# Four stores of the next-to-last output chunk: from two issuing engines to three

## The chip, the cores and the metric

The kernel runs on one core of one Trainium2 chip. The metric is the device time of one execution in microseconds (us), as the median of several runs. A profile of one further execution gives the times of single instructions. The engines are named as in the profile: PE is TensorE's matrix multiplication and PEld its weight load, DVE is VectorE, ACT is ScalarE, POOL is GpSimd, SP is SyncE, which here only issues transfers and waits. A "q" behind the name (SPq, ACTq, POOLq) stands for the engine's sequencer, which waits, branches and issues transfers.

## The reference

Two blocks follow each other. For 8 batches, 8 heads, 576 tokens and 64 features per head:

```python
kv = np.einsum('bhsd,bhse->bhde', k, v)
out = np.einsum('bhsd,bhde->bhse', q, kv)
rms = np.sqrt(np.mean(out * out, axis=-1, keepdims=True) + 1e-06)
x = (out / rms * g_norm)                      # then heads are put side by side: (8, 576, 512)

gate_pre = sum(conv_w[k] * xp[:, k:k + S, :] for k in range(5))   # xp: x with 4 zero rows ahead
gate = 1.0 / (1.0 + np.exp(-gate_pre))
result = (gate * (x @ w_val)) @ w_out         # float32, (8, 576, 512)
```

## The kernel before, in words

The kernel is a list of small steps, written out by hand as the string PLAN (lines 19 to 227) and carried out one after the other by the loop at lines 881 to 887. Each step's name is one of the functions above that loop, its numbers are that function's arguments, and the numbers behind an "@" choose buffers. Every engine executes its own instructions in the order in which the steps issue them; between engines, semaphores hold an instruction back until what it reads or overwrites is ready. These waits are put in by the framework. So the order of PLAN is the order on each engine, and a transfer that an engine issues stands in that engine's line like any other instruction.

The last part of the work is the product with w_out. Batches are handled in pairs i = 0 to 3; a pair's 2 x 576 tokens make eight chunks of 128 tokens and a ninth chunk (number 8) for the two remainders of 64. Two neighbouring chunks (2p and 2p + 1) are computed together by seven fast_product steps (line 819, matmuls at line 838), a scheme that saves one of eight block products. Each fast_product adds into a PSUM bank, and fast_keep (line 842) brings the banks into the output tiles ot (128 x 512 values in float32, four buffers) by ScalarE copies (lines 850 to 854 and 861) and VectorE additions (line 848, and line 861 as a VectorE copy for the very last one). Step fast_keep 3 3 5 is the addition that completes chunk 6 of the last pair, fast_keep 3 3 6 the copy that completes chunk 7.

An ot tile goes to memory in four transfers of 32 rows each (64 KB): store (line 866) loops over the blocks j = 0 to 3 that it is given and issues each on the queue that it is given (line 870). Nearly all chunks go through SyncE. Chunk 8 of the last pair goes through store_side (line 872), that is GpSimd; it stands some steps ahead of the end. Chunks 6 and 7 of the last pair go through store_last (line 863), which splits the four blocks between SyncE and ScalarE: with n = 1 blocks 2 and 3 on ScalarE, with n = 0 blocks 0 and 1 on SyncE. The last steps of the plan are:

```python
fast_keep 3 3 1 @ 0; fast_product 3 3 5; fast_keep 3 3 4; fast_product 3 3 6; fast_keep 3 3 5;
store_last 3 6 1; store_last 3 6 0; fast_keep 3 3 6; store_last 3 7 1; store_last 3 7 0
```

So each of the two engines issues two stores of chunk 6 and two stores of chunk 7. Transfers of SyncE and ScalarE share a set of eight semaphores, those of GpSimd have eight of their own; each transfer in turn takes the next semaphore of its set and waits, if it must, until the semaphore's former transfer has landed.

After the last step the program leaves the framework's context (line 913). There every engine executes a DRAIN and reports; SyncE first waits until every transfer has landed; GpSimd, after its own DRAIN, gathers the reports of the other engines, releases them, clears the semaphores, and gathers once more.

Of the kernel before, what the change touches and what calls it, by code (L numbers as in the profile page):

```python
# [222 lines left out]
fast_keep 3 3 0 @ 1; store_side 3 8; fast_product 3 2 6; fast_keep 3 2 5; fast_product 3 3 2; fast_keep 3 2 6;  # L223
store 3 4; fast_product 3 3 1 @ 0; fast_keep 3 3 2; fast_product 3 3 3; fast_product 3 3 4; store 3 5;
fast_keep 3 3 1 @ 0; fast_product 3 3 5; fast_keep 3 3 4; fast_product 3 3 6; fast_keep 3 3 5;
store_last 3 6 1; store_last 3 6 0; fast_keep 3 3 6; store_last 3 7 1; store_last 3 7 0
"""


# [1 line left out]
def kernel(  # L231
# [11 lines left out]
    nc = tc.nc  # L243
# [12 lines left out]
    HB = P // TB  # L256
# [603 lines left out]
            last = (i, p) == (B // 2 - 1, 2 * NV - 1)  # L860
            (nc.vector.tensor_copy if last else nc.scalar.copy)(out=second[:, LOW], in_=a)

    def store_last(i, c, n):
        store(i, c, nc.scalar if n else nc.sync, range(n * HB // 2, (n + 1) * HB // 2))

    def store(i, c, queue=nc.sync, blocks=range(HB)):
        ot = st["ot", i, c]
        for j in blocks:
            bb, n = divmod(c * HB + j, NJ * HB) if c < 2 * NJ else (j // 2, NJ * HB + j % 2)
            queue.dma_start(out=rows_out[2 * i + bb, n], in_=ot[j * TB:(j + 1) * TB, :])  # L870

    def store_side(i, c):
# [5 lines left out]
        turn_x, keep_x, turn_blocks, move_blocks, halo, gate_start, gate_tap, gate_end, val_product, keep_val, gated,  # L878
        val_sums, x_sums, val_fast, val_keep, out_product, keep_out, weight_sums, token_sums, fast_product, fast_keep,
        store, store_side, store_last)}  # L880
    with tc.manual_schedule():
        set_up()
# [35 lines left out]
```

## Time and profile before

| what | value |
| --- | --- |
| time, median of 3 runs | 295.73 us (295.55 to 296.74) |
| span of the profiled execution, first to last instruction | 294.9 us |
| mean granted TensorE clock | 0.993 |
| PE busy | 287.0 us, 97% of the span |
| DVE busy | 268.7 us, 91% |
| ACT busy | 198.7 us, 67% |
| POOL busy | 120.7 us, 41% |
| stores from ot on SyncE, whole kernel | 136, median 1.7 us from issue to landing |
| the same on GpSimd | 4, median 2.1 us |
| the same on ScalarE | 4, median 2.0 us |

The profiled execution's own time is told by its span, 294.9 us; the median of the runs lies 0.83 us above it. In the profile's rows the first numbers of a timeline line are the start (counted from the span's start) and the length in us; in brackets stands how long the engine had been idle, and what ended that. In the rows of a group, "x4: 315/396/430, 290.4 to 291.7" means four instructions with the shortest, median and longest duration in ns, and the start of the first and of the last in us. Rows by stretches give the busy time of each engine, then the granted clock, the busy share of the DMA engines and the GB/s moved. The duration of a transfer's issue (DMA_DIRECT2D) is the engine's time to issue it; when its data has landed is given as "DMA to landing".

### The profile page before, as it was taken

To read this page: it belongs to the slowest core of one execution; us is meant where nothing else is said; L and a number is where in the kernel's file an instruction comes from. 1 tells how busy PE (TensorE), PEld (TensorE's weight loads), DVE (VectorE), ACT (ScalarE), POOL (GpSimd) and SP (SyncE) were. 2 spreads that over 40 slices of the span, in tenths; PEclk is the share of its full clock that TensorE was granted. 3 is DMA by queue.
4 is the path that set the end of the run, shared out by engine and by line. 5 is a ranking of instruction groups with operands and counts; after the bars stand their busy time and mean duration, and the time that the engine had idled before them with its cause. 6 is when DMAs were issued, how large, how long until landed. Compare 5 with 4: busy or idle time off the path is not lost.

```text
span 294.9 us, 8675 instructions
## 1 busy us (share of the span) xinstructions
PE 287.0 (97%) x3279; PEld 226.9 (77%) x3279; DVE 268.7 (91%) x483; ACT 198.7 (67%) x621; POOL 120.7 (41%) x131
## 2 busy tenths in 40 slices
PE   7999999999999999999999999999999999999994
PEld 3776878788887768878887767888887588788583
DVE  1699999999999999999999999999998999999812
ACT  2899999999786667867477576659588433723330
POOL 3067054854491477421881649021592072000020
PEclk9997999999999999999999999999999999999999
DMA  7999998886686766946789789534553170221344
GB/s 268 379 392 410 284 276 230 239 258 176 197 189 198 234 150 182 341 144 174 182 237 279 167 218 308 165 112 109 141 128 80 44 170 2 57 53 36 98 105 120
DMA packets 32009, 55.51 MB, mean 188 GB/s; under 512 B 6166, under 2 KB 14358, under 8 KB 31968
## 3 DMA queue, kind: packets, MB, share of 16 engines
q1 hardware_dynamic: 29328, 49.50, 57.2%
q0 software_dynamic: 1760, 3.43, 5.2%
q10 hardware_dynamic: 880, 2.03, 1.8%
q8 instruction: 26, 0.43, 0.6%
q14 instruction: 15, 0.12, 0.1%
HBM read 39.21 MB, written 9.44 MB: 165 GB/s over the span
## 4 chain that ended last, share of the span: by engine, by line
PE 94%; DMA 2%; ACT 1%; DVE 1%; issue 0%
PE bank L838 33%; PE bank L747 28%; PE bank L698 11%; PE bank L476 7%; PE bank L551 6%; PE bank L785 5%; PE bank L648 2%; DMA qs<-in_q_dram 2%; PE bank L563 2%; PE bank L515 1%; PE bank L464 0%; ACT wexp L409 0%; DVE x L626 0%; ACT sq L596 0%; DVE ss L607 0%; ACT wexp L407 0%
## 5 line engine op out<-in xcount | busy, mean ns | idle before, releaser
L617 POOL TENSOR_TENSOR rt<-ss,mhalf 128x8 f32<-128x8 f32 (+3 forms) x38 | 73.1, 1937 | 82.0 <-DVE ss L607 81.8
L686 DVE SCALAR_TENSOR_TENSOR gate<-xT,cwT,gate 128x576 f32<-128x576 f32 x128 | 100.4, 807 | 0.2
L636 ACT ACTIVATE x<-bank,rt 128x64 f32<-128x64 f32 x252 | 56.1, 375 | 3.5 <-POOL rt L617 3.2
L838 PE MATMUL bank<-wsum,w 128*128 128x256 f32 x192 | 47.3, 381 | 0.0
L669 POOL DMA_DIRECT2D xT<-y x48 | 26.6, 559 | 41.6 <-DVE gv L754 13.5
L838 PEld LDWEIGHTS bank<-wsum,w 128*128 128x128 f32 x192 | 36.0, 190 | 6.1 <-issue 0.8
L747 PE MATMUL bank<-xs,vsum 128*128 128x288 f32 x144 | 37.1, 407 | 0.0
L747 PEld LDWEIGHTS bank<-xs,vsum 128*128 128x128 f32 x144 | 27.3, 190 | 7.3
L698 PE MATMUL bank<-xT,wval 128*128 128x288 f32 x128 | 32.8, 411 | 0.0
L838 PE MATMUL bank<-wout,gv 128*128 128x256 f32 x128 | 32.3, 382 | 0.0
L698 PEld LDWEIGHTS bank<-xT,wval 128*128 128x128 f32 x128 | 24.0, 192 | 6.3
L693 ACT ACTIVATE gate<-gate 128x576 f32<-128x576 f32 x32 | 23.0, 727 | 7.9 <-DVE gate L686 7.8
L838 PEld LDWEIGHTS bank<-wout,gv 128*128 128x128 f32 x128 | 24.0, 190 | 3.5
L680 ACT ACTIVATE gate<-xT,cwT 128x576 f32<-128x576 f32 x32 | 25.2, 804 | 0.9 <-DVE gv L711 0.9
L747 PE MATMUL bank<-xT,wval 128*128 128x288 f32 x96 | 25.7, 406 | 0.0
L600 ACT ACTIVATE sq<-bank 128x256 f32<-128x256 f32 (+1 forms) x70 | 21.6, 400 | 6.0 <-PE bank L551 5.8
L711 DVE TENSOR_TENSOR gv<-gv,gate 128x576 f32<-128x576 f32 x32 | 23.5, 745 | 2.0 <-ACT gate L693 1.5
L607 DVE TENSOR_REDUCE ss<-sq 128x8 f32<-128x520 f32 (+1 forms) x40 | 24.7, 624 | 0.5 <-ACT sq L600 0.4
L848 DVE TENSOR_TENSOR ot<-bank,ot 128x256 f32<-128x256 f32 (+1 forms) x32 | 17.2, 546 | 8.4 <-PE bank L838 4.1
L747 PEld LDWEIGHTS bank<-xT,wval 128*128 128x128 f32 x96 | 18.2, 190 | 4.5
L854 ACT COPY ot<-bank 128x256 f32<-128x256 f32 x16 | 6.0, 376 | 22.6 <-PE bank L838 22.6
L551 PEld LDWEIGHTS bank<-kv,qT 64*64 64x64 f32 x1008 | 16.3, 135 | 4.8 <-issue 2.1
(91 smaller groups left out, 469.4 us busy)
## 6 DMA issues: line engine op xcount, KB each, us to landing
qs<-in_q_dram SPq DMA_DIRECT2D x96, 140.0 KB, 4.0
out_dram<-ot SPq DMA_DIRECT2D x136, 64.0 KB, 1.7
k<-in_k_dram SPq DMA_DIRECT2D x14, 576.0 KB, 4.9
v<-in_v_dram SPq DMA_DIRECT2D x12, 576.0 KB, 5.3
xT<-y POOLq DMA_DIRECT2D x48, 64.0 KB, 2.7
xT<-y SPq DMA_DIRECT2D x48, 64.0 KB, 2.7
y<-in_moe_w_val_dram SPq DMA_DIRECT2D x4, 512.0 KB, 11.9
w<-in_moe_w_out_dram SPq DMA_DIRECT2D x4, 512.0 KB, 7.1
```

The lines of the kernel that those rows point to most:

```text
L551: nc.tensor.matmul(st["raw", b, c][r][cols, to * D:(to + 1) * D], st["qT", b][rows, hp, first:first + D], kvs[b % 2][rows, hp, :], start=T ...
L607: nc.vector.reduce_sum(out=st["ss", b][:, FIRST[c]:FIRST[c] + n], in_=st["sq", b, c][:, 0:n], axis=AX.X)
L617: nc.gpsimd.tensor_tensor(out=st["rt", b][:, which], in0=st["ss", b][:, which], in1=mhalf[:, which], op=ALU.pow)
L636: nc.scalar.activation(out=x[:, to * D:(to + 1) * D], in_=raw[:, h * D:(h + 1) * D], func=AF.Copy, scale=root[:, to:to + 1])
L669: (nc.sync if i % 2 else nc.gpsimd).dma_start(out=xTs[b % 2][i * TB:(i + 1) * TB, :, first:first + P], in_=y[a * TB:(a + 1) * TB, i])
L680: nc.scalar.activation(out=gate[:], in_=xTs[b % 2][:, jt, HALO:SX], func=AF.Copy, scale=cwT[:, K - 1, jt:jt + 1])
L686: nc.vector.scalar_tensor_tensor(out=gate[:], in0=xTs[b % 2][:, jt, tap * TB:tap * TB + S], scalar=cwT[:, tap, jt:jt + 1], in1=gate[:], op ...
L693: nc.scalar.activation(out=gate[:], in_=gate[:], func=AF.Sigmoid)
L698: nc.tensor.matmul(val[:], wval[:, kc, jt * P:(jt + 1) * P], xTs[b % 2][:, kc, HALO + n * SV:HALO + (n + 1) * SV], start=(kc == 0), stop=( ...
L711: nc.vector.tensor_tensor(out=both, in0=both, in1=st["gate", b, jt][:], op=ALU.mult)
L747: nc.tensor.matmul(st[bank, "val", b, mj][:], weights_[:, k], tokens()[:, k], start=(n in (0, 1, 3) and k == 0), stop=(k == NK // 2 - 1), ...
L838: nc.tensor.matmul(st[bank, i, p], tokens()[:, k], weights_[:, k], start=(n < 2 and k == 0), stop=(k == NK // 2 - 1), skip_group_check=True)
```

## The change

PLAN's last line becomes two, and store_last takes the engine's number and the range of blocks as arguments, with GpSimd as a third engine. Of chunk 6, blocks 2 and 3 are now issued by GpSimd, block 1 by ScalarE and block 0 by SyncE. Chunk 7 is stored as before: blocks 2 and 3 on ScalarE, 0 and 1 on SyncE.

```diff
-store_last 3 6 1; store_last 3 6 0; fast_keep 3 3 6; store_last 3 7 1; store_last 3 7 0
+store_last 3 6 2 2 4; store_last 3 6 1 1 2; store_last 3 6 0 0 1; fast_keep 3 3 6; store_last 3 7 1 2 4;
+store_last 3 7 0 0 2
...
-    def store_last(i, c, n):
-        store(i, c, nc.scalar if n else nc.sync, range(n * HB // 2, (n + 1) * HB // 2))
+    def store_last(i, c, n, first, last):
+        store(i, c, (nc.sync, nc.scalar, nc.gpsimd)[n], range(first, last))
```

HB is 4, the number of blocks in a chunk. All lines behind the plan move down by one: line 870 becomes 871, and line 913 becomes 914.

## The prediction

> **What bounds the kernel now.** I read three views: the page's slices (who is busy when), the timeline of the last 12 us, and the groups of the end line L913 (what the engines do after their last instruction of the kernel's own). First two parts of the page:
>
> ```profile
> PE 287.0 (97%) x3279; PEld 226.9 (77%) x3279; DVE 268.7 (91%) x483; ACT 198.7 (67%) x621; POOL 120.7 (41%) x131
> PE   7999999999999999999999999999999999999994
> POOL 3067054854491477421881649021592072000020
> ```
>
> PE is busy in every slice but the first and half of the last, so TensorE bounds the kernel up to its last matmul. The change touches nothing before that, so its whole price lies in the tail. POOL is idle in the last slices but one; that is the free engine that the change uses. The timeline of the tail:
>
> ```profile
> 283.53 0.39 ACT L850 COPY ot<-bank 128x256 f32<-128x256 f32 x1
> ...
> 283.94 2.06 POOL L870 DMA_DIRECT2D out_dram<-ot  x4 [36.82 <-ACT ot L850]
> ...
> 289.49 1.03 PE L838 MATMUL bank<-wsum,gv 128*128 128x256 f32 x4
> 289.69 0.69 DVE L848 TENSOR_TENSOR ot<-bank,ot 128x512 f32<-128x512 f32 x1 [0.38 <-DMA out_dram<-ot]
> 290.46 1.80 ACTq L870 DMA_DIRECT2D out_dram<-ot  x4
> 290.56 0.42 DVE L861 COPY ot<-bank 128x256 f32<-128x256 f32 x1 [0.17 <-PE bank L838]
> ```
>
> Chunk 6 is ready when the DVE addition ends (289.69 + 0.69 = 290.38), chunk 7 when the DVE copy ends (290.56 + 0.42 = 290.98). Behind them stand eight 64 KB stores, four on SyncE and four on ScalarE. The timeline of SyncE alone has its four in one row; then the group of all eight, and the one for ScalarE's last:
>
> ```profile
> 290.45 1.72 SPq L870 DMA_DIRECT2D out_dram<-ot  x4
> ```
> ```profile
> L870 SPq DMA_DIRECT2D out_dram<-ot x4: 315/396/430, 290.4 to 291.7; - x4
> L870 ACTq DMA_DIRECT2D out_dram<-ot x4: 371/410/440, 290.5 to 291.8; - x4
> ...
> DMA to landing us min/median/max: 1.7/1.9/2.1
> ```
> ```profile
> L870 ACTq DMA_DIRECT2D out_dram<-ot x1: 440/440/440, 291.8 to 291.8; - x1
> ...
> DMA to landing us min/median/max: 2.1/2.1/2.1
> ```
>
> Each queue takes about 0.4 us per store, so the last is issued at 291.8 and lands 2.1 us later, at 293.9. What follows is the exit, all of line L913, from 283 us to the end:
>
> ```profile
> L913 SPq EVENT_SEMAPHORE  x11: 17/28/28, 292.2 to 294.8; - x11
> L913 POOLq EVENT_SEMAPHORE  x4: 17/17/17, 294.1 to 294.8; - x4
> L913 POOLq DRAIN  x3: 40/108/5310, 285.3 to 294.6; - x3
> L913 SPq DRAIN  x3: 7/7/7, 294.1 to 294.4; - x3
> L913 PEldq DRAIN  x2: 13/604/1195, 289.4 to 294.4; - x2
> ```
>
> SyncE waits for every landing and reports at 294.1; POOL, which gathers the reports of all engines, takes over at 294.1 (its first semaphore) and the span ends at 294.9. So 0.8 us of exit stand behind the last report. The row to stop at is POOL's DRAIN. One of the three takes 5310 ns. The same view cut to POOL and 284 to 291 us has it alone:
>
> ```profile
> L913 POOLq DRAIN  x1: 5310/5310/5310, 285.3 to 285.3; - x1
> ```
>
> It runs from 285.3 to 290.6, whereas POOL's last store issue ended at 283.94 + 2.06 = 286.00. It waits for no semaphore that the trace shows, and lasts 4.6 us past the end of POOL's last issue. The other two (108 and 40 ns, after 294) follow no store. Now this drain ends 3.5 us before 294.1 and costs nothing. The changed kernel puts two POOL stores ahead of it, at the very end.
>
> **The change part by part.** *Removed:* one store of chunk 6 from SyncE and one from ScalarE, the last of each queue's pair. In the built program each queue then has three stores: one of chunk 6, two of chunk 7. The first goes out as before (290.45, 290.46); the next must wait for chunk 7's copy, 290.98, plus the 0.07 us that lay between the addition's end (290.38) and SyncE's first issue (290.45): 291.05. Another 0.43 us for one issue (1.72 for four) puts the last at 291.48 in place of 291.8, and with the same 2.1 us to land it is down at 293.6: 0.3 us earlier than 293.9.
>
> *Added, the stores:* two issues on POOL of this kind:
>
> ```profile
> L870 POOL DMA_DIRECT2D out_dram<-ot x4: 498/504/567, 283.9 to 285.5; - x4
> ...
> DMA to landing us min/median/max: 2.0/2.1/2.4
> ```
>
> The first takes 0.57, the second 0.50, 1.07 together. When do they start? In the changed program POOL waits for DVE's addition in a separate semaphore instruction, then issues. The nearest place where a POOL store stands behind such a wait is L669; its group from 198 to 211 us:
>
> ```profile
> L669 POOL DMA_DIRECT2D xT<-y x3: 551/551/599, 209.7 to 210.8; - x3
> L669 POOLq EVENT_SEMAPHORE  x1: 11006/11006/11006, 198.1 to 198.1; - x1
> ```
>
> The wait ends at 198.1 + 11.0 = 209.1, the first issue begins at 209.7: a lead of about 0.55 us. The other bound is the store of chunk 8, which began at 283.94, right when the ACT copy before it had ended (283.53 + 0.39 = 283.92): no visible lead. I take 0.55, the like case: the wait ends at 290.4, the issues run from 290.95 to 292.0, and the second, begun at 291.5, lands 1.9 to 2.4 us later, 293.4 to 293.9. So the landings end between 293.6 and 293.9: at best 0.3 us is won, and no more, since the DMA engines are not idle meanwhile (the busy share by stretches):
>
> ```profile
> 291.50:292.00 0.50, 0.00 (x0) 0.00 (x0) 0.00 (x0) 0.00 (x0) 0.00 (x0) 1.00 0.94 262
> 292.00:292.50 0.50, 0.00 (x0) 0.00 (x0) 0.00 (x0) 0.00 (x0) 0.00 (x0) 1.00 0.89 262
> 292.50:293.00 0.50, 0.00 (x0) 0.00 (x0) 0.00 (x0) 0.00 (x0) 0.00 (x0) 1.00 0.92 275
> ```
>
> The Trainium skill, "DMA: Bandwidth & Descriptors", section "Specifications", gives about 1 us to the first byte for a GpSimd store and about 0.6 us for one of SyncE or ScalarE, which speaks against the move. By that figure, as an estimate, each moved store would land 0.4 us later after its issue. The trace has 2.1 against 1.9 us at the median, half of it; the rows decide, and the sum changes by 0.2 us in its unimportant part.
>
> *Added, the wait behind them:* queued behind the two issues on POOL is only the exit: the drain, then the gathering of all reports. Until now its cover was the 3.5 us between 290.6 and 294.1. That cover goes. The drain's price behind a late store is bounded below by its short forms, 0.04 to 0.1 us (nothing outstanding), and above by 5.3 us from its own start. I take 4.6 us past the last issue, from the one drain that follows stores. Counted the other way, from the last POOL landing (285.5 + 2.4 = 287.9, so 2.7 us to 290.6), it gives 293.4 to 293.9 plus 2.7, that is 296.1 to 296.6: the same place within 0.5 us.
>
> *Sum:* last POOL issue ends 292.0; drain to 296.6; exit 0.8; span 297.4 against 294.9, +2.5 us. The runs' median, 295.73, lies 0.83 us above the span; I carry that over: 298.2 us. With no lead on POOL the drain ends at 296.0 and the time is 297.6; with the lead and another half microsecond in drain or landing it is 298.7. Its own range is 297.4 to 298.8.
>
> **The rivals.**
>
> *The drain has no price of its own* (not slower). Then the long DRAIN at 285.3 would have ended for some other reason, and the end of the matmuls at 290.5 is suspiciously near its end at 290.6. For this: one sample only, and no semaphore. Against: PE has a drain of its own (1195 ns from 289.4) for its matmuls, POOL has none to wait for, and POOL's short drains, which come where no store is open, last 0.1 us. The mechanism left is the relief of the issuing queues, and the place where it decides is the last landing: 0 to 0.3 us earlier than 293.9, so 295.4 to 295.7 us. It decides if POOL's drain ends before 294.1, that is if it costs less than 2.1 us past the last issue. The Trainium skill has this side too: "DMA: Bandwidth & Descriptors", section "Issuing engines are not separate DMA queues", says that issuing from several engines saves just the time to issue, which is usually small. The trace agrees on the landings: 0.3 us is all that can go.
>
> *The drain works off a backlog, so much per store.* Four stores from 283.94 to the drain's end at 290.6 make 6.6 us, or 1.7 us each; two would make 3.3 us from 290.95, ending at 294.3, 0.2 us after the present gathering: 295.9 us. For this: POOL's own issues follow each other unhindered, so whatever remains is done behind them. Against: after the last landing at 287.9 no store is left to work on, and the drain still lasts 2.7 us.
>
> *The drain is longer here*, since the two POOL stores share the DMA engines with six others, all in 290.4 to 294: every microsecond of it goes into the time, 299 us or more.
>
> That the change does nothing is ruled out: the two POOL stores do stand behind chunk 8's four in the built program, and chunk 7's queues are as before.
>
> **How the numbers follow.** About 0.5% (1.5 us) is what a measurement of this kernel can tell from no change. The fixed drain: 0.68, 298.2 us. The longer one: 0.04. The backlog: 0.13, 295.9. No price: 0.15, 295.4 to 295.7. Slower by over 0.5% (above 297.2) are the first two, 0.72. The other two lie within 0.5%; a gain of 1.5 us would need the last landing at 292.4, when the stores of chunk 7 are barely issued, so 0.01 for faster and 0.27 for the same. The range that leaves out 2 in 10 takes in the forecast's own and reaches down over the backlog: 295.8 to 298.8 us.
>
> **What would show it.** In the profile after, on POOL: two more L871 issues starting at 290.9 or 291.0 (a start at 290.4 takes away the lead); a DRAIN on L914 that ends near 296.6, and POOL's gathering semaphore right behind it rather than at SyncE's report. SyncE's last wait should end at 293.7 to 294.1, well before. If the drain again ends at about 290.6 or right after the issues, the first rival holds; near 294.3, the second. If SyncE's report comes after POOL's drain, the forecast is wrong whatever the time.

## The result and the profile after

The changed kernel takes 298.31 us (median of 6 runs, 298.04 to 299.62) against 295.5 us for the kernel before (6 runs, 295.27 to 296.74). The ratio is 1.0092, with a 95% interval of 1.007 to 1.0114: it is slower by 2.1 to 3.4 us.

First the same two rows of the page, then the timeline of the tail (start, length, engine, line, what; lines are one higher than before):

```profile
PE   7989999999999999999999999999999999999990
POOL 3066064654694289224770756040890262000021
```
```profile
288.72 0.69 DVE L849 TENSOR_TENSOR ot<-bank,ot 128x512 f32<-128x512 f32 x1 [0.38 <-DMA out_dram<-ot]
289.49 1.40 ACTq L871 DMA_DIRECT2D out_dram<-ot  x3
289.59 0.42 DVE L862 COPY ot<-bank 128x256 f32<-128x256 f32 x1 [0.17 <-PE bank L839]
289.96 0.98 POOL L871 DMA_DIRECT2D out_dram<-ot  x2 [4.94 <-issue]
```

PE's last slice has gone from 4 to 0: a whole slice of 7.4 us now passes with hardly a matmul. The addition that completes chunk 6 ends at 288.72 + 0.69 = 289.41, while it ended at 290.38 in the profile of before. This 1.0 us ahead of the change's first instruction is not the change's. The profiled execution here took 298.27 us for its 296.5 us span, 1.8 us more; that of before, with its 294.9 us, was one of about 296.7 us by the same distance, as the slowest of its runs was. What that of before lost, it lost early: from 24.3 to 27.7 us the TensorE clock granted to it was 0.50, in the execution here 1.00 (the third number from the end; first the row of before). Its matmuls run 0.3 us late ahead of this stretch, 1.8 us behind it, and 1.0 us late at the end.

```profile
24.30:27.70 3.40, 3.40 (x78) 2.81 (x77) 3.40 (x8) 3.34 (x9) 3.37 (x5) 0.50 1.04 413
```
```profile
24.30:27.70 3.40, 3.40 (x83) 2.84 (x83) 3.40 (x8) 3.34 (x8) 3.09 (x5) 1.00 1.03 412
```

So the spans differ by 1.6 us only, and the comparison has to be made from the addition on. From there to the end of the span it was 294.9 - 290.38 = 4.5 us; it is now 296.45 (the trace's last event) - 289.41 = 7.0 us.

The group of the exit's line, and below it the eight stores of chunks 6 and 7:

```profile
L914 SPq EVENT_SEMAPHORE  x11: 17/28/156, 292.2 to 296.4; - x11
L914 POOLq EVENT_SEMAPHORE  x4: 17/17/17, 295.7 to 296.3; - x4
L914 POOLq DRAIN  x3: 40/108/5298, 290.4 to 296.2; - x3
L914 SPq DRAIN  x3: 7/7/7, 293.0 to 295.9; - x3
```
```profile
L871 SPq DMA_DIRECT2D out_dram<-ot x3: 314/314/417, 289.5 to 290.4; - x3
L871 ACTq DMA_DIRECT2D out_dram<-ot x3: 370/374/432, 289.5 to 290.5; - x3
L871 POOL DMA_DIRECT2D out_dram<-ot x2: 496/497/498, 290.0 to 290.4; - x2
...
DMA to landing us min/median/max: 1.6/2.0/2.4
```

SyncE has seen every landing and reports at 293.0, and the same row of before had 294.1: measured from the addition, 3.65 us now against 3.73 us. So the stores themselves are 0.1 us earlier. But POOL's DRAIN stands from 290.4 to 295.7, and POOL's first gathering semaphore comes right behind it at 295.7. From there the exit takes the same 0.8 us. From SyncE's report to the drain's end are 2.6 us; less the 0.1 us of the stores, that is the 2.5 us.

### The profile page after: what moved, and what is told of

Read it like the earlier page. It is cut to its first block, busy times and chain, and to the rows that moved or that the text cites. A ratio compares the mean times of both kernels' runs of the same rounds, so it can differ in the third digit from the quotient of the medians.

```text
span 296.5 us, 8676 instructions
## 1 busy us (share of the span) xinstructions
PE 285.7 (96%) x3279; PEld 225.4 (76%) x3279; DVE 268.5 (91%) x483; ACT 198.4 (67%) x621; POOL 123.0 (41%) x133
## 3 DMA queue, kind: packets, MB, share of 16 engines
q0 software_dynamic: 1824, 3.56, 5.2%
## 4 chain that ended last, share of the span: by engine, by line
PE 74%; DVE 9%; ACT 9%; DMA 3%; issue 2%; POOL 1%; SPq 0%; POOLq 0%; DVEq 0%; ACTq 0%
PE bank L839 30%; PE bank L748 28%; PE bank L786 5%; PE bank L477 4%; DVE gate L687 4%; PE bank L552 3%; ACT x L637 3%; DMA qs<-in_q_dram 2%; PE bank L564 2%; DMA out_dram<-ot 1%; POOL rt L618 1%; DVE ss L608 1%; DVE ot L423 1%; ACT gv L708 1%; PE bank L516 1%
## 5 line engine op out<-in xcount | busy, mean ns | idle before, releaser
L871 POOL DMA_DIRECT2D out_dram<-ot x6 | 3.0, 510 | 41.8 <-ACT ot L851 36.8
```

## The experiments

What has to be told apart is what this drain's length hangs on. **Theory A** is that of the prediction: a fixed price past POOL's last issue. **Theory C** counts a fixed price from the last landing. **Theory B** came up with the two traces side by side: before, the drain lasted 4.563 us past the end of the last issue, after it 4.728 us, and POOL issues 55 transfers in the first kernel and 57 in the second (48 block moves, 3 small loads at the start, 4 or 6 stores). 4.563 / 55 and 4.728 / 57 are both 0.083 us. All times of a drain to the third decimal, and all landings, are read from the traces' event times; the rows give the start to 0.1 us. A diff of PLAN shows only the steps of a line that matter, without the rest of the line.

### An early drain in the changed kernel

```diff
+    def drain_side():
+        nc.gpsimd.drain()
...
-fast_keep 2 3 4; halo 7; val_keep 6 0 6;
+fast_keep 2 3 4; halo 7; drain_side; val_keep 6 0 6;
```

> The changed kernel with one more DRAIN on POOL, put behind POOL's last compute step of the loop (the halo copies of batch 7, about 247 us), where POOL then idles for 35 us. Theory A (the price is fixed): the exit's drain still ends 4.6 to 4.8 us past POOL's last issue, and the ratio to the kernel before stays at about 1.009. Theory B (the drain walks through every transfer that POOL issued since its last drain, 4.56 us for 55 in the kernel before and 4.73 us for 57 in the changed one, 0.083 us each): the early drain takes 51 x 0.083 = 4.2 us where nobody waits, the exit's drain 6 x 0.083 = 0.5 us past the last issue, and the time falls back to that of before or 0.1 us below, ratio 0.998 to 1.001. Theory C (the drain ends 2.7 to 2.9 us past the last landing): as theory A.

Measured: 295.52 us (12 runs) against 295.54 us, ratio 0.9994 (0.9983 to 1.0004). The price is gone, with the two late stores on POOL still in place. The early drain and POOL's last work before it:

```profile
L874 POOLq DRAIN  x1: 6347/6347/6347, 244.1 to 244.1; - x1
```
```profile
244.08 2.07 POOL L677 COPY xT<-xT 128x124 f32<-128x124 f32 x4 [2.89 <-ACT xT L656]
```

POOL's copies end at 246.15, the drain at 250.4: 4.25 us for 51 transfers, the last of which POOL had issued at about 240. Nobody waits for it. Then the tail:

```profile
289.97 0.98 POOL L871 DMA_DIRECT2D out_dram<-ot  x2 [4.93 <-issue]
```
```profile
L917 POOLq DRAIN  x3: 46/107/2741, 290.4 to 293.6; - x3
L917 SPq DRAIN  x3: 7/7/7, 293.0 to 293.4; - x3
```
```profile
L871 POOL DMA_DIRECT2D out_dram<-ot x2: 496/496/496, 290.0 to 290.5; - x2
...
DMA to landing us min/median/max: 2.2/2.3/2.4
```

The exit's drain ends at 290.4 + 2.74 = 293.1, within 0.1 us of SyncE's report. That is 2.2 us past the last issue and not the 0.5 us of theory B: POOL's last store, begun at 290.45, lands 2.4 us later, at 292.8, and the drain ends 0.3 us after that. So theory A falls, theory B holds for the count, and it lacked a floor: the drain does not end before the last landing. Theory C, which has 2.7 us past the landing, falls too.

### The early drain in the kernel before

The same two edits in the kernel before.

> The kernel before with the same early DRAIN on POOL. All theories: the time of before, ratio 0.998 to 1.002, since the exit's drain is hidden either way. What tells them apart is that drain's length past POOL's last issue: 4.6 us by theory A, 4 x 0.083 = 0.3 us by theory B, 2.7 us past the last landing by theory C.

Measured: 295.58 us against 295.54 us, ratio 1.0 (0.9986 to 1.0015).

```profile
L916 POOLq DRAIN  x3: 51/108/2824, 284.4 to 293.8; - x3
```

The drain ends at 284.4 + 2.82 = 287.2, 2.1 us past the last issue (285.16) and 0.2 us past the last POOL landing (287.04). The 4.6 us past the issue have gone, against theory A, and so have the 2.7 us past the landing of theory C. Theory B's 0.3 us was wrong, as before, by the floor.

### One late store in place of two

```diff
-store_last 3 6 2 2 4; store_last 3 6 1 1 2; store_last 3 6 0 0 1; fast_keep 3 3 6;
+store_last 3 6 2 3 4; store_last 3 6 1 1 3; store_last 3 6 0 0 1; fast_keep 3 3 6;
```

> The changed kernel with one store of chunk 6 on POOL in place of two (block 3; ScalarE takes blocks 1 and 2). Theories A and B: the exit's drain is as long as with two (4.6 to 4.7 us past the last issue), which comes 0.5 us earlier, so 2.0 us instead of 2.5 us over the tail of before, ratio 1.006 to 1.008. A price per late store would halve the drain and end it at about the present report of SyncE: ratio 1.000 to 1.002.

Measured: 297.64 us against 295.54 us, ratio 1.0072 (1.0047 to 1.0098).

```profile
291.31 0.50 POOL L871 DMA_DIRECT2D out_dram<-ot  x1 [4.94 <-issue]
```
```profile
L914 POOLq DRAIN  x3: 40/108/5163, 291.3 to 297.0; - x3
```

The drain ends 4.646 us past the issue: 56 x 0.083. A price per late store is ruled out; from the addition (290.77) to the end (297.24) are 6.5 us in place of 7.0, shorter by about the issue that POOL doesn't make.

### A late copy and no late store

```diff
+    def touch_side(i, c):
+        nc.gpsimd.tensor_copy(out=warm[:], in_=st["ot", i, c][:, 0:1])
...
-store_last 3 6 1; store_last 3 6 0; fast_keep 3 3 6;
+store_last 3 6 1; store_last 3 6 0; touch_side 3 6; fast_keep 3 3 6;
```

> The kernel before with all stores where they were, and one tiny POOL copy (128x1, its result is not used) that waits for the addition that completes chunk 6, so that POOL reaches its exit only then, with no late POOL store. Theory A, with the price counted from the last issue, and theory C: the 4.6 us are over by then, the drain ends within 0.2 us of the copy, and the ratio is 1.000. Theory B, or any price that is work which begins with the drain: the drain takes 4.6 us from the copy's end at about 290.7 and ends near 295.2, 1.1 us after the present gathering: ratio 1.003 to 1.005.

Measured: 296.87 us against 295.54 us, ratio 1.0046 (1.003 to 1.0061).

```profile
290.40 0.19 POOL L873 COPY warm<-ot 128x1 f32<-128x1 f32 x1 [4.53 <-DVE ot L848]
```
```profile
L916 POOLq DRAIN  x3: 40/107/4778, 290.4 to 295.7; - x3
L916 SPq DRAIN  x3: 7/7/7, 293.9 to 295.4; - x3
```

No store is late here; the last POOL store was issued 4.5 us before the copy and has long landed. Still the drain takes 4.58 us from the copy's end and ends at 295.2, 1.2 us after SyncE's report. So it is not a time that runs from the last issue: it begins only when POOL has come to the drain. One late copy on POOL is enough to expose it. How much is exposed depends on when that instruction ends: the copy ends 0.3 us after the addition and lengthens the tail from 4.5 to 5.7 us, the changed kernel's two issues end 1.5 us after the addition and lengthen it to 7.0 us.

### 24 tiny transfers more, long before the end

```diff
+    def tiny_side():
+        for n in range(24):
+            nc.gpsimd.dma_start(out=rooms["wexp"][0][0:1, n * 16:(n + 1) * 16], in_=g_norm.unsqueeze(0)[:, 0:16])
...
-fast_keep 2 3 4; halo 7; val_keep 6 0 6;
+fast_keep 2 3 4; halo 7; tiny_side; val_keep 6 0 6;
```

> The changed kernel with 24 more POOL transfers of 64 bytes each (their result is not used), issued around 247 us where POOL is idle; all have landed long before the end. The four runs before this left a drain of 0.083 us for each POOL transfer since the last drain, but not less than until 0.2 to 0.3 us past the last landing. If the count of transfers is what is paid: 81 x 0.083 = 6.7 us past the last issue, 2.0 us more than in the changed kernel, ratio 1.015 to 1.017. If bytes or packets are paid (24 transfers of 64 bytes add almost none): 4.7 to 4.9 us, ratio 1.009. If only transfers that are still in flight are paid: as the second.

Measured: 300.09 us against 295.52 us, ratio 1.0158 (1.0128 to 1.0188).

```profile
L875 POOL DMA_DIRECT2D wexp<-in_g_norm_dram x24: 484/484/556, 247.0 to 258.0; - x24
```
```profile
L918 POOLq DRAIN  x3: 40/112/7255, 291.3 to 299.1; - x3
L918 SPq DRAIN  x3: 7/7/7, 293.9 to 298.8; - x3
```

The drain is 7255 ns in place of 5298 ns: 1957 ns for 24 transfers, 0.082 us each, though each moves 64 bytes in place of 64 KB and is over 30 us before the end. So neither bytes nor what is still in flight sets the price. Packets are another matter. The expectation had the tiny transfers add almost none, and that is not so, as the row of POOL's DMA queue shows (packets, MB, share of the DMA engines), first in the changed kernel, then here:

```profile
q0 software_dynamic: 1824, 3.56, 5.2%
```
```profile
q0 software_dynamic: 2592, 3.57, 5.2%
```

The 24 tiny transfers add 768 packets, 32 each, and the 57 others make 1824 / 57 = 32 each on average. In these kernels a count of transfers and a count of packets can't be told apart; what follows says transfers.

### Two stores of chunk 5 on POOL

```diff
 (on the kernel before, with the changed kernel's store_last)
-store 3 5;
+store_last 3 5 2 2 4; store_last 3 5 0 0 2;
...
-store_last 3 6 1; store_last 3 6 0; fast_keep 3 3 6; store_last 3 7 1; store_last 3 7 0
+store_last 3 6 1 2 4; store_last 3 6 0 0 2; fast_keep 3 3 6; store_last 3 7 1 2 4; store_last 3 7 0 0 2
```

> Two stores of chunk 5 on POOL instead of two of chunk 6, which go back to SyncE and ScalarE; 57 POOL transfers as in the changed kernel. POOL's last issue then ends some 2 us after its chunk 8 stores, at about 287.0 in the time of the kernel before, and the drain 57 x 0.083 = 4.7 us later, at 291.8, before SyncE's report at 294.1: no price, ratio 0.998 to 1.002. A theory by which late or more POOL stores cost something by themselves (contention of their transfers, longer landings) would still show 0.2 us or more over before.

Measured: 295.69 us against 295.52 us, ratio 1.0004 (0.9989 to 1.0019).

```profile
282.96 3.08 POOL L870 DMA_DIRECT2D out_dram<-ot  x6 [36.83 <-ACT ot L850]
```
```profile
L913 POOLq DRAIN  x3: 40/108/5295, 285.5 to 293.7; - x3
L913 SPq DRAIN  x3: 7/7/7, 293.2 to 293.5; - x3
```

POOL's last issue ends at 286.0. This is the expected 287.0 in the time of the kernel before, since this profile reaches the addition 1.0 us sooner (289.41 against 290.38). The two stores follow POOL's four of chunk 8 without a lead, as POOL's wait was over before their turn came, and so they end 1 us after them and not the "some 2 us" of the expectation. The drain is the same (57 transfers, 4.73 us past the last issue), but it ends at 290.8, 2.4 us before SyncE's report: covered, and nothing is paid. By this sum POOL's last work must end 4.7 us before SyncE's report if nothing is to be paid; here it ends 7.2 us before.

### The block moves on SyncE

```diff
-            (nc.sync if i % 2 else nc.gpsimd).dma_start(
+            nc.sync.dma_start(
                 out=xTs[b % 2][i * TB:(i + 1) * TB, :, first:first + P],
```

> The changed kernel with the 48 block moves of POOL (xT<-y, spread over 77 to 241 us) on SyncE instead, so that POOL issues 9 transfers in all. By count: 9 x 0.083 = 0.75 us, so the exit's drain ends 0.2 to 0.3 us past the last landing of POOL, some 2.2 us past its last issue, as with the early drain, and the tail from chunk 6's addition to the end is 4.5 us again instead of 7.0. If the price hung on the late stores alone, the drain would stay at 4.7 us. What the moves cost on SyncE in the body is open (its queue is busier by 48 issues of 0.4 us): the time may lie 0 to 6 us above that of before for that reason, so the verdict is read from the tail.

Measured: 315.16 us against 295.52 us, ratio 1.0656 (1.0624 to 1.0688). The moves cost 19.6 us in all, far more than the 0 to 6 us that I had left open; why was not followed up. The tail answers the question all the same:

```profile
307.16 0.69 DVE L849 TENSOR_TENSOR ot<-bank,ot 128x512 f32<-128x512 f32 x1 [0.38 <-DMA out_dram<-ot]
```
```profile
L914 POOLq DRAIN  x3: 40/103/2891, 308.8 to 312.2; - x3
L914 SPq DRAIN  x3: 7/7/7, 311.5 to 312.0; - x3
```

With 9 POOL transfers in the kernel the drain ends at 311.7, 0.4 us past POOL's last landing (311.29) and 0.2 us after SyncE's report; the span ends at 312.5, 4.6 us after the addition, where it was 4.5 us in the kernel before. Two late stores of POOL are nearly free when POOL issued little before them.

### All drains in one table

| kernel | POOL transfers since the last drain | drain's end past POOL's last instruction, us | us per transfer |
| --- | --- | --- | --- |
| early drain, behind the copies that end at 246 us | 51 | 4.25 | 0.083 |
| before | 55 | 4.56 | 0.083 |
| late copy | 55 | 4.58 | 0.083 |
| one late store | 56 | 4.65 | 0.083 |
| changed | 57 | 4.73 | 0.083 |
| chunk 5 | 57 | 4.73 | 0.083 |
| tiny transfers | 81 | 6.69 | 0.083 |
| early drain, exit of the changed kernel | 6 | 2.18 | last landing + 0.29 |
| early drain, exit of the kernel before | 4 | 2.09 | last landing + 0.21 |
| moves on SyncE | 9 | 2.32 | last landing + 0.42 |

## Why the prediction was right, and where its reason was not

**The place.** Right: PE's work ahead of the tail is untouched, and the end is set by POOL's drain, with the gathering semaphore right behind it at 295.7 and SyncE's report 2.6 us earlier. The 1.0 us between the two profiles taken off, every sign that the prediction named came: POOL's issues from 290.9, SyncE's report at 294.0, the drain's end at 296.6.

**The start of POOL's stores.** The lead of 0.55 us between the end of POOL's wait and its first issue is 0.50 us in the changed kernel: its wait, below, begins at 284.29, ends at 289.45, and the first issue begins at 289.96. The issues took 0.98 us in place of 1.07: the first of the two was not the slower one.

```profile
L871 POOLq EVENT_SEMAPHORE  x1: 5167/5167/5167, 284.3 to 284.3; - x1
```

**The drain.** 4.73 us past the last issue where the sum had 4.6. Together with the exit: 2.5 us more in the tail, as predicted; the time, 298.31 us, lies 0.1 us above the forecast. The 0.83 us that the prediction added to the span compared an execution with runs that it didn't belong to (the distance is 1.8 us), but both kernels have the same distance, so it dropped out of the sum. That the time came so near is in part luck: over the six runs of before, with their median of 295.5 us, the change costs 2.8 us, 0.3 us more than the sum had, and the 295.73 us of the first three runs, on which the sum was built, made up for most of that.

**The reason.** The step "in the one drain that follows stores" gave the right size and the wrong kind, and the size was luck: the change takes the number of POOL's transfers from 55 to 57 only, so a price that was read off as fixed came out 0.17 us short. The price is not fixed and does not belong to the late stores: it is 0.083 us for each of the 57 transfers that POOL has issued in the whole kernel, 51 of them some 50 us or more before the end, and it falls due when POOL reaches its drain. The rival of a backlog had the kind right (so much per transfer), but it charged 1.7 us to each of the four last stores; the drain of the changed kernel, as long with two late stores as with four early ones, ruled that out. It was argued there that no store was left to work on after the last landing: the late copy and the tiny transfers show that landed transfers are charged as well. POOL's short drains (108 and 40 ns), which the prediction put down to no store being open, come with no transfer since the long drain just before them.

**The drain without a price.** Ruled out. That its end in the kernel before fell on the end of the matmuls was chance: in the changed kernel it ends 6.3 us after the addition, and so well after the last matmul.

**The relief of the queues.** 0 to 0.3 us were predicted for the landings. Counted from the addition, ScalarE's last store lands 0.3 us earlier, as the sum had it. But POOL's second store now lands last, 2.4 us after its issue (1.9 to 2.4 had been taken), and so SyncE's report comes only 0.1 us earlier. With the drain's price taken out (the early drain), the ratio is 0.9994 with 1 in its interval, so no gain can be told. The Trainium skill, "DMA: Bandwidth & Descriptors", section "Issuing engines are not separate DMA queues", has DMAs issued from several engines save only the time to issue them; these runs agree in that nothing more was gained.

**What stays open.** What the drain does in its 0.083 us per transfer isn't seen in a trace; the runs show the count on which it depends, that an earlier drain resets it, and that it does not end before the last landing. That the 24 tiny transfers cost 0.082 us each says that it isn't bytes. Whether transfers or packets are counted is open, since all of POOL's transfers here came to 32 packets each. The end behind the last landing is not a fixed distance either: 0.21, 0.29 and 0.42 us with 4, 6 and 9 transfers, which rises by 0.042 us per transfer, half of 0.083. So a part of the price may fall due only after the last landing; these are three points, and no run was made to test it.

## What to carry to other kernels

Look at POOL's DRAIN in the exit before giving POOL anything late: if POOL's last instruction, a store or a copy, ends less than the drain's length before SyncE reports the last landing, the rest of that length is added to the time. The length comes from the number of POOL's transfers in the whole kernel, so it can be paid earlier: one explicit drain in a stretch where POOL idles took the 2.5 us away here. And compare two profiles from the change's first instruction on, not by their spans.

## What the runs showed of the hardware that I had not expected

- A POOL DRAIN took 0.083 us for each transfer that POOL had issued since its last drain (4.25 us for 51, 6.69 us for 81), whether long landed or not and whether of 64 bytes or 64 KB (32 packets on average in either case). With few transfers it ended 0.21, 0.29 and 0.42 us past the last landing (4, 6 and 9 transfers).
- It began to count only when POOL got there: behind a copy at 290.4 us, when POOL's last transfer had landed at 287.8, it took 4.58 us.
- After a wait in an instruction of its own, POOL began a store 0.50 us later (289.45 to 289.96), where SyncE needed 0.03 us (289.45 to 289.48).
